# One tile's masks ahead of attention, and a planner that reckons with instruction supply and a halved clock

## The chip, the cores and the metric

The kernel runs on one core of a Trainium2 chip. The metric is device time in microseconds (us), the median of three runs. The engines are PE (matrix products, with PEld for its weight loads), DVE (vector), ACT (scalar), POOL (GpSimd) and SP, which only issues DMA transfers here.

## The reference

Sliding-window attention with sink tokens, then two MLPs, all in f32:

```python
scores = scale * q @ k^T                    # B=2, H=8, S=768, D=64
keep = (pos_k < n_sink) | ((0 <= rel) & (rel < window))     # n_sink=4, window=128
a = softmax(where(keep, scores, -1e9)); attn = a @ v        # -> x: 1536 tokens x 512
h = x @ w_in;  y = (h * clip(h + 3, 0, 6) / 6) @ w_out      # first MLP, d_ff = 2048
h = y @ w_in2; out = (h * sigmoid(1.702 * h)) @ w_out2      # second MLP
```

## The kernel before, in words

**Tiles.** Attention is cut into 12 tiles of 128 query tokens, T0 to T11. Each tile has two *duos* of four heads, so there are duos 0 to 23. For a duo PE makes the scores (L1381), DVE adds a mask and takes the row minimum of the negated scores (L1396, into a `pexp` buffer), ACT takes the exponential and its row sum (L1404), DVE inverts the sums (L1412, L1413), DVE or ACT scales each head (L1423 or L1421), PE transposes in two *turns* (L1432) and ACT or DVE copies each turn into a `pts` buffer (L465, L467). After both duos PE multiplies with the values (L1455, L1463), and ACT and DVE split the result into `xyh + xyl` (L465, L1482). [...] There are eight `pexp` buffers, which is one tile's worth, and eight PSUM banks in all.

**MLPs.** MLP products use f32 numbers split into two rounded parts, three products each. An *item* is 512 tokens by 128 columns of `w_in` (12 records of L1158, then the gate, then 12 of L1207). Weights come packed through two `stage` buffers and are converted by ACT (L495) and DVE (L500, L508, L516, L523); a stage buffer can be loaded again once L523 has read it. Eight `items` of the first MLP run on the first 512 tokens, that is on T0 to T3, while the later tiles' attention is still being done.

**Masks.** T0 uses mask 0, T1 mask 1, T2 to T5 mask 2, and the second batch alike. All three are written before attention begins, from iotas and the two parameters.

**The planner.** The program is straight-line code under manual scheduling. `Plan.op` collects operations with an engine, a cost in ns, buffers and a due time; `Plan.issue` runs through them as a list scheduler, keeps a clock for each engine, picks the next operation by its earliest start and its due time, and emits it. So its constants (`SLACK`, `HOLD`, `MARGIN`, `RAMP`, `PAIR`, ...) set each engine's order of instructions. The engines then run these orders strictly, with semaphores. SP too is one queue in order: a load that waits for its buffer holds up every load behind it.

```python
start, o, cost = min((c for c in best[eng] if c[0] <= soon), key=lambda c: c[1].due)
...
if eng == "PE":
    if o.tiled != tiled:
        start += ENTER if o.tiled else LEAVE
        tiled = o.tiled
end = start + cost
```

Of the kernel before, what the change touches and what calls it, by code (L numbers as in the profile page):

```python
# [9 lines left out]
F32 = mybir.dt.float32  # L10
# [4 lines left out]
ALU = mybir.AluOpType  # L15
PSUM = bass.MemoryType.PSUM

P = 128
SINKS = 4
HALF = 64  # L20
# [14 lines left out]
NVC = 3  # L35
SLACK = 50
HOLD = 425
MARGIN = 18538
LONG = 1000
ENTER = 100  # L40
LEAVE = 200
STICK = 88113
WAIT = 5
ISSUE = 1300
ADD_DMA = 4500
PACT = 0.09
PDVE = 0.51
STRETCH = 1.0
LATER = 1000000
H_BANKS = 3  # L50
RAMP0 = 8045
RAMP = 1654
PAIR = 4384
PAIR2 = 5887
DOWN = 7072
START = 592
RATE = 1.56
RATE2 = 1.21
NU = 3
# [16 lines left out]
def tile_sink_window_attention_moe_moe2(  # L76
# [10 lines left out]
    nc = tc.nc  # L87
# [12 lines left out]
    W = P + TAIL  # L100
# [31 lines left out]
    def load_kq(T):  # L132
        nc.sync.dma_start(out=kqt[T], in_=kq[T])
# [17 lines left out]

    const.tile([P, 88], F32, name="gap_x")
    xy = const.tile([P, 2, 2 * NBLK * NC * 256 + APART], F32R, name="xy")
# [86 lines left out]
    const.tile([P, 72], F32, name="gap_w")  # L240
    with tc.tile_pool(name="msk", bufs=1) as mp:
        grid = mp.tile([P, P], F32, name="grid")
        nc.gpsimd.iota(grid, pattern=[[-1, P]], base=0, channel_multiplier=1, allow_small_or_imprecise_dtypes=True)
        colc = mp.tile([P, HALF], F32, name="colc")
        nc.gpsimd.iota(colc, pattern=[[1, HALF]], base=0, channel_multiplier=0, allow_small_or_imprecise_dtypes=True)
        far = mp.tile([P, P], F32, name="far")
        nc.gpsimd.iota(far, pattern=[[-1, P]], base=P, channel_multiplier=1, allow_small_or_imprecise_dtypes=True)
        t0 = mp.tile([P, P], F32, name="t0")
        out_of = mp.tile([P, P], F32, name="out_of")
        snk = mp.tile([P, HALF], F32, name="snk")  # L250
        nos = mp.tile([P, HALF], F32, name="nos")
        nc.gpsimd.memset(masks[0], LOW)
        nc.vector.tensor_scalar(out=t0, in0=grid, scalar1=0.0, scalar2=None, op0=ALU.is_lt)
        range_check()
        fast = nc.values_load(flag[0:1, 0:1], min_val=0, max_val=1)
        window_of_params()
        top, low, keys, own, ends = slice(0, HALF), slice(HALF, P), slice(HALF, P), slice(P, P + HALF), slice(P + HALF, W)
        first_sinks, rest = slice(P, P + SINKS), slice(P + SINKS, W)
        at = lambda out, grid, op, x: nc.vector.tensor_scalar(
            out=out, in0=grid, scalar1=x, scalar2=LOW, op0=op, op1=ALU.mult  # L260
        )
        times = lambda out, in_: nc.vector.tensor_scalar(out=out, in0=in_, scalar1=LOW, scalar2=None, op0=ALU.mult)

        nc.vector.scalar_tensor_tensor(out=out_of, in0=grid, scalar=win, in1=t0, op0=ALU.is_ge, op1=ALU.max)
        at(snk, colc, ALU.is_ge, nsk)
        times(masks[1][:, keys], out_of[:, :HALF])
        times(masks[0][low, own], out_of[low, HALF:])
        nc.vector.tensor_tensor(out=masks[0][:, keys], in0=masks[1][:, keys], in1=snk, op=ALU.max)
# [7 lines left out]
        nc.vector.tensor_tensor(out=masks[1][top, rest], in0=masks[2][top, rest], in1=nos[top, :], op=ALU.min)  # L276

        nc.vector.tensor_copy(masks[2][:, : P + SINKS], masks[1][:, : P + SINKS])
        nc.vector.tensor_copy(masks[2][low, rest], masks[1][low, rest])

# [18 lines left out]
    class Op:  # L299
        pass  # L300

    class Plan:
# [19 lines left out]
        def op(self, opts, fn, due, reads=(), writes=(), adds=(), chain=None, after=()):  # L322
            o = Op()
            o.opts, o.fn, o.due = opts, fn, LATER if due is None else due
            o.deps, o.order, o.finish, o.eng = [], list(after), None, None
            o.tiled = chain == "scores" or opts[0][1] == 1830
            for b in reads:
                o.deps += b.writers
# [45 lines left out]
        def issue(self):  # L374
# [20 lines left out]
            ready = [o for o in self.ops if not need[id(o)]]  # L395
            at = dict.fromkeys(ENG, 0)
            tiled = True
            while ready:
                best = {}
                for o in ready:  # L400
                    placed = self.place(o)
                    if placed is None:
                        continue
                    t = placed[0]
                    pick = None
                    for eng, cost in o.opts:
                        x = max(t, at[eng])
# [14 lines left out]
                if eng == "PE":  # L422
# [865 lines left out]
    def mlp_rings(plan, pool, psum):  # L1288
# [7 lines left out]
        for cls, n, cols, dt in (  # L1296
            ("w0h", 2, 512, F32R), ("w0l", 2, 512, F32R), ("u", NU, 512, F32), ("aside", 4, 512, F32),
        ):
            plan.ring(cls, n, lambda k, cls=cls, cols=cols, dt=dt: pool.tile([P, cols], dt, name=cls, tag=f"{cls}{k}"))
        spare = [t.rearrange("p h d -> p (h d)") for t in vb]  # L1300
# [18 lines left out]
    def plan_attention(plan, pool, due):  # L1319
# [23 lines left out]
        def load(T):  # L1343
            if ("kq", T) not in landed:
                plan.op([("SP", 532480 / RATE_DMA)], lambda e: load_kq(T), None, writes=[kq_b[T]])
            if ("vb", T) not in landed:
# [4 lines left out]
        def duo(d, pts):  # L1351
# [37 lines left out]
            )  # L1389
            heads = [(a, j) for a in range(2) for j in range(2)]  # L1390
            for a, j in heads:
                n = 2 * a + j
# [7 lines left out]
                    when, reads=[sc[j], mask_b[kind]], writes=[pes[n], nbs[n]],  # L1400
                )
                plan.op(
                    [("ACT", 443)],
# [333 lines left out]
```

## Time and profile before

| | |
|---|---|
| time, median of 3 runs (lowest to highest) | 573.64 us (573.54 to 573.85) |
| the profiled execution: its time, its span | 575.76 us, 573.9 us |
| PE, DVE, ACT busy share of the span | 97%, 84%, 70% |
| mean granted clock of PE | 0.985 |

The span runs from the first to the last instruction; what lies around it in the profiled execution is 575.76 - 573.9 = 1.9 us. Busy shares are averages over very different stages: the first 60 us are attention with a few items, from there to about 564 us PE has work without a break.

### The profile page before, as it was taken

To read this page: it belongs to the slowest core of one execution; us is meant where nothing else is said; L and a number is where in the kernel's file an instruction comes from. 1 tells how busy PE (TensorE), PEld (TensorE's weight loads), DVE (VectorE), ACT (ScalarE), POOL (GpSimd) and SP (SyncE) were. 2 spreads that over 40 slices of the span, in tenths; PEclk is the share of its full clock that TensorE was granted. 3 is DMA by queue.
4 is the path that set the end of the run, shared out by engine and by line. 5 is a ranking of instruction groups with operands and counts; after the bars stand their busy time and mean duration, and the time that the engine had idled before them with its cause. 6 is when DMAs were issued, how large, how long until landed. Compare 5 with 4: busy or idle time off the path is not lost.

```text
span 573.9 us, 11897 instructions
## 1 busy us (share of the span) xinstructions
PE 559.1 (97%) x4626; PEld 501.4 (87%) x4626; DVE 481.7 (84%) x1039; ACT 400.9 (70%) x855; POOL 63.9 (11%) x70
## 2 busy tenths in 40 slices
PE   6898999999999999999999999999999999999996
PEld 6787888888888888889999888888888888999996
DVE  6779999999997669999999999999666655667785
ACT  6779779846675678578765565765478788768762
POOL 0000000000000203000000000000003334765000
PEclk9769999999999999999999999999999999999999
DMA  8956364324334515112222142324034467999512
GB/s 263 381 196 196 129 211 166 101 90 135 133 131 152 106 49 100 38 73 74 75 75 97 50 147 94 127 73 148 0 93 73 74 107 145 168 184 199 100 38 79
DMA packets 27824, 69.89 MB, mean 122 GB/s; under 512 B 2736, under 2 KB 15024, under 8 KB 23664
## 3 DMA queue, kind: packets, MB, share of 16 engines
q1 hardware_dynamic: 15248, 53.06, 27.2%
q0 software_dynamic: 12224, 15.73, 17.4%
q8 instruction: 38, 0.62, 0.4%
q10 hardware_dynamic: 288, 0.26, 0.2%
q14 instruction: 26, 0.21, 0.1%
HBM read 47.02 MB, written 3.15 MB: 87 GB/s over the span
## 4 chain that ended last, share of the span: by engine, by line
PE 92%; ACT 4%; DMA 1%; issue 1%; DVE 0%; DVEq 0%; ACTq 0%
PE bank L1207 29%; PE bank L1158 21%; PE bank L954 13%; PE bank L650 13%; PE bank L738 7%; PE bank L1432 3%; PE bank L1381 3%; PE bank L1455 2%; PE bank L1463 2%; DMA stage<-in_w_dram 1%; ACT pexp L1404 1%; ACT pts L465 1%; ACT pexp L1421 0%; ACT wf L495 0%; ACT u L1170 0%
## 5 line engine op out<-in xcount | busy, mean ns | idle before, releaser
L1207 PE MATMUL bank<-wg 128*128 128x512 f32 x768 | 187.5, 381 | 0.0
L1207 PEld LDWEIGHTS bank<-wg 128*128 128x128 f32 x768 | 142.4, 189 | 19.0
L1158 PE MATMUL bank<-xy,w0h 128*128 128x512 f32 x384 | 116.3, 384 | 1.6 <-ACT pts L465 0.9
L1158 PEld LDWEIGHTS bank<-xy,w0h 128*128 128x128 f32 x384 | 71.1, 189 | 12.0 <-ACT pts L465 1.2
L1158 PE MATMUL bank<-xy,w0l 128*128 128x512 f32 x192 | 72.8, 379 | 0.0
L465 ACT CAST wg<-wf 128x512 fp32r<-128x512 f32 x80 | 49.1, 617 | 31.4 <-PE bank L1207 24.1
L902 POOL DMA_DIRECT2D wf<-wf x24 | 29.0, 1300 | 229.0 <-ACT wf L883 193.1
L1404 ACT ACTIVATE pexp<-pexp,nb 128x196 f32<-128x196 f32 x96 | 43.1, 452 | 10.7 <-DVE nb L1396 10.6
L578 DVE TENSOR_TENSOR wg<-wf,wg 128x512 fp32r<-128x512 f32 x64 | 43.7, 684 | 3.1 <-ACT wg L465 3.1
L578 DVE TENSOR_TENSOR w0l<-wf,w0h 128x512 fp32r<-128x512 f32 x60 | 40.9, 682 | 3.3 <-ACT w0h L465 3.1
L495 ACT ACTIVATE wf<-stage 128x1024 f32<-128x1024 f32 x32 | 38.0, 1188 | 6.0 <-DMA stage<-in_w_dram 5.9
L1158 PEld LDWEIGHTS bank<-xy,w0l 128*128 128x128 f32 x192 | 36.3, 189 | 5.1
L593 DVE TENSOR_TENSOR wg<-u,wg 128x512 fp32r<-128x512 f32 x56 | 38.0, 683 | 1.2 <-ACT wg L465 0.7
L523 DVE SCALAR_TENSOR_TENSOR wf<-stage,wf 128x1024 int32<-128x1024 int32 x32 | 38.9, 1216 | 0.1
L516 DVE SCALAR_TENSOR_TENSOR wf<-stage,wf 128x1024 int32<-128x1024 int32 x32 | 38.9, 1215 | 0.1
L650 PE MATMUL bank<-xy,w0h 128*128 128x512 f32 x128 | 38.1, 379 | 0.0
L604 ACT ACTIVATE u<-bank 128x512 f32<-128x512 f32 x32 | 19.1, 596 | 27.2 <-PE bank L1158 20.1
L465 ACT CAST wg<-u 128x512 fp32r<-128x512 f32 x47 | 29.0, 622 | 8.5 <-DVE u L1175 5.6
L1170 ACT ACTIVATE u<-bank,three 128x512 f32<-128x512 f32 x32 | 21.8, 682 | 16.4 <-PE bank L1158 16.2
L1432 PE MATMUL bank<-ident,pexp 128*128 128x128 f32 x192 | 29.6, 293 | 3.7 <-DVE pexp L1423 2.9
L1396 DVE CUSTOM_DVE_ANT_0 pexp<-bank,mask 128x196 f32<-128x196 f32 x96 | 29.9, 354 | 1.1 <-PE bank L1432 0.7
L1432 PEld LDWEIGHTS bank<-ident,pexp 128*128 128x128 f32 x192 | 23.7, 149 | 8.1 <-issue 2.6
(245 smaller groups left out, 1234.3 us busy)
## 6 DMA issues: line engine op xcount, KB each, us to landing
stage<-in_w_dram SPq DMA_DIRECT2D x32, 1024.0 KB, 4.9
wf<-wf POOLq DMA_DIRECT2D x24, 256.0 KB, 3.8
wf<-in_kq_dram SPq DMA_DIRECT2D x8, 520.0 KB, 11.2
vc<-in_vc_dram SPq DMA_DIRECT2D x12, 320.0 KB, 3.5
vb<-in_v_dram SPq DMA_DIRECT2D x10, 256.0 KB, 5.1
kept<-in_kq_dram SPq DMA_DIRECT2D x4, 520.0 KB, 10.3
vc<-xy SPq DMA_DIRECT2D x7, 256.0 KB, 2.6
vc<-xy POOLq DMA_DIRECT2D x7, 256.0 KB, 4.7
```

The lines of the kernel that those rows point to most:

```text
L465: eng.copy(out, in_)
L495: lambda e: e.activation(w.tile.bitcast(F32), top.bitcast(F32), AF.Abs),
L516: lambda e: e.scalar_tensor_tensor(out=w.tile, in0=top, scalar=-0x40000000, in1=w.tile, op0=ALU.bitwise_and, op1=ALU.bitwise_or),
L523: lambda e: e.scalar_tensor_tensor(out=w.tile, in0=low, scalar=29, in1=w.tile, op0=ALU.logical_shift_right, op1=ALU.bitwise_or),
L578: lambda e: e.tensor_tensor(out=lo.tile[at], in0=of(), in1=hi.tile[at].bitcast(F32), op=ALU.subtract),
L650: e.matmul(bank.tile, l, woven(r), start=(begin and j == 0 and k == 0), stop=(j == 1 and k == 2), skip_group_check=True,)
L738: e.matmul(bank.tile[:, :256], l, woven(r), start=(begin and j == 0 and k == 0), stop=(j == 1 and k == 2), skip_group_check=True,)
L954: e.matmul(to, l, woven(t), start=(begin and n == 0 and m == 0 and e4 % share == 0), stop=(n == pairs - 1 and m == 2), skip_group_check=True,)
L1158: e.matmul(h.tile[:, :n], w, woven(x), start=(c == 0 and k == 0), stop=(c == NC - 1 and k == 2))
L1207: e.matmul(yb.tile, l, woven(r), start=(begin and k == 0), stop=(end is not None and k == 2))
L1404: lambda e, n=n: e.activation(pes[n].tile[:, :W], pes[n].tile[:, :W], AF.Exp, bias=nbs[n].tile, scale=-1.0, accum_out=z.tile[:, n : n + 1],),
L1432: e.transpose(pt.tile[:, n * P : (n + 1) * P], pes[2 * a + j].tile[:, x * P : (x + 1) * P], ident)
```

## The change

**Masks.** Before attention DVE now writes only mask 0 (with the key columns of mask 1, from which mask 0 is made). The rest of mask 1 (`second_mask`, 7 instructions) and mask 2 (`third_mask`, 2) become planned operations of DVE after duo 0's comparisons. One comparison (`t0`) goes from DVE to POOL. The mask work space moves from a pool of its own to slot 0 of the `aside` ring.

**Planner.** It counts the instructions passed by PE and lets PE stop when a fetched block is used up (`FETCHED`, `CHUNK`, `FETCH`, `FETCH_BUSY`); it doubles the cost of PE work in a stretch behind much idle time (`idle`, `slow`); DVE's clock starts at `MASKED`; loads of k and q from tile 7 on are not issued before `KQ_AT + (T - 7) * KQ_STEP`. The other constants and the order of the first loads are new.

```diff
-    ("kq", 0), ("kq", 1), ("vb", 0), ("vc", 0), ("w", 0), ("vb", 1), ("vc", 1), ("kq", 2), ("vb", 2), ("vc", 2), ("kq", 3),
-    ("w", 1),
+    ("kq", 0), ("vb", 0), ("kq", 1), ("vc", 0), ("vc", 1), ("vb", 1), ("w", 0), ("kq", 2), ("vb", 2), ("vc", 2), ("kq", 3), ("w", 1),
...
-SLACK = 50
-HOLD = 425
-MARGIN = 18538
+SLACK = 54
+MASKED = 5700
+HOLD = 597
+MARGIN = 20604
...
+CHUNK = 252
+FETCHED = 443
+FETCH = 2800
+FETCH_BUSY = 6300
+LATE_KQ = 7
+KQ_AT = 53230
+KQ_STEP = 5947
...
-        nc.vector.tensor_scalar(out=t0, in0=grid, scalar1=0.0, scalar2=None, op0=ALU.is_lt)
+    nc.gpsimd.tensor_scalar(out=out_of, in0=grid, scalar1=0.0, scalar2=None, op0=ALU.is_lt)
...
+                    if start > at[eng] > 6000:
+                        idle.append((at[eng], start))
+                    passed += o.count
+                    if passed > edge:
+                        seen = start + cost * (edge - passed + o.count) / o.count
+                        if coming > seen:
+                            idle.append((seen, coming))
+                            cost += coming - seen
+                            seen = coming
+                        coming = seen + (FETCH_BUSY if self.dma_free > seen + 1500 else FETCH)
+                        edge += CHUNK
+                    while idle and idle[0][1] < idle[-1][1] - 4300:
+                        idle.pop(0)
+                    if idle and sum(b - a for a, b in idle) > 2100:
+                        a = idle[0][0] + 2900
+                        slow = (a, max(a, idle[-1][1]) + 3500)
+                        idle.clear()
+                    cost += max(0, min(slow[1] - max(start, slow[0]), 2 * (start + cost - max(start, slow[0]))) / 2)
...
+                o = plan.op([("SP", 532480 / RATE_DMA)], lambda e: load_kq(T), None, writes=[kq_b[T]])
+                if T >= LATE_KQ:
+                    o.not_before = KQ_AT + (T - LATE_KQ) * KQ_STEP
...
+            if d == 0:
+                plan.op([("DVE", 1300)], lambda e: second_mask(), when, writes=mask_b[1:2], after=seen)
+                plan.op([("DVE", 400)], lambda e: third_mask(), when, reads=mask_b[1:2], writes=mask_b[2:], after=seen)
```

**What moves.** PE, behind T0's four turns (`pts` and `vb_63`, `vc_66` are T0's). Before, T0's values come next, then the scores of duos 4 and 5 (of each kind of row one stands here), then T1's turns:

```order
L1432 MATMUL bank<-ident,pexp 128x128 x16
L1455 MATMUL bank<-pts,vb_63 64x128 x2
L1463 MATMUL bank<-pts,vc_66 64x64 x4
...
L1381 MATMUL bank<-wf 64x64 x8
L1381 MATMUL bank<-wf 64x68 x4
...
L1432 MATMUL bank<-ident,pexp 128x128 x16
```

Of the change, in the same place:

```order
L1479 MATMUL bank<-ident,pexp 128x128 x16
L1422 MATMUL bank<-wf 64x64 x8
L1422 MATMUL bank<-wf 64x68 x4
...
L1502 MATMUL bank<-pts,vb_63 64x128 x2
L1510 MATMUL bank<-pts,vc_66 64x64 x4
...
L1479 MATMUL bank<-ident,pexp 128x128 x16
```

So the scores of T2 go ahead of T0's values. What follows has the same blocks in both kernels as far as T1's values: T1's turns, duos 6 and 7, T1's values. Up to the first long run of L1158 (L1194 in the change), two more turns stand ahead of it in the change: 18 against 16.

SP, behind the branch. Before (`wf` and `kept` take k and q of tiles 4 on, `stage` takes weights, `vb` and `vc` the values):

```order
L133 DMA wf<-in_kq_dram 128x1040 x4
L133 DMA kept<-in_kq_dram 128x1040
L143 DMA vb_63<-in_v_dram 128x512
L133 DMA kept<-in_kq_dram 128x1040 x2
L149 DMA vc_66<-in_vc_dram 80x1024
L143 DMA vb_64<-in_v_dram 128x512
L127 DMA stage_60<-in_w_dram 128x2048
L149 DMA vc_67<-in_vc_dram 80x1024
L143 DMA vb_65<-in_v_dram 128x512
L127 DMA stage_61<-in_w_dram 128x2048
```

Of the change:

```order
L140 DMA wf<-in_kq_dram 128x1040 x3
L134 DMA stage_60<-in_w_dram 128x2048
L150 DMA vb_63<-in_v_dram 128x512
L156 DMA vc_66<-in_vc_dram 80x1024
L150 DMA vb_64<-in_v_dram 128x512
L134 DMA stage_61<-in_w_dram 128x2048
L156 DMA vc_67<-in_vc_dram 80x1024
```

Three loads of k and q stand there instead of seven; those of tiles 7 to 10 come later, one by one among the weight loads. The third weight tile now stands ahead of T3's values, the fourth ahead of the second part of T4's.

DVE, from duo 0's reciprocal on (`z_249` is duo 0's row sums, `z_318` duo 1's, `aside0` now holds the iotas). The rows with `mask1`, `mask2` and `gap_x` are the moved mask work; left out are a multiplication and two copies. Of the change:

```order
L1460 RECIPROCAL z_249<-z_249 128x4
L265 TENSOR_SCALAR mask1_123<-aside0_126,par_121 128x64
L265 TENSOR_SCALAR mask2_124<-aside0_126,par_121 64x64
L265 TENSOR_SCALAR gap_x_69<-aside0_126,par_121 64x64
...
L283 TENSOR_TENSOR mask1_123<-mask2_124,gap_x_69 64x64
L1470 TENSOR_SCALAR pexp_177<-pexp_177,z_249 128x196
L1470 TENSOR_SCALAR pexp_178<-pexp_178,z_249 128x196
L286 COPY mask2_124<-mask1_123 128x132
L287 COPY mask2_124<-mask1_123 64x64
L1459 TENSOR_SCALAR z_318<-z_318 128x4
```

Before, these nine mask instructions stood ahead of the first comparison, and the reciprocal was followed at once by the four scalings of duo 0 (L1423).

## Rows read from the trace of the kernel before

**Rows 1.** Busy us of PE, PEld, DVE, ACT, POOL by stretch; granted clock, DMA share, GB/s.

```profile
6.60:13.50 6.90, 4.10 (x183) 3.60 (x179) 6.10 (x37) 5.29 (x21) 0.00 (x0) 1.00 1.04 320
13.50:20.30 6.80, 6.48 (x110) 6.03 (x113) 4.94 (x24) 5.31 (x18) 0.00 (x0) 0.50 1.03 343
20.30:27.10 6.80, 4.50 (x156) 4.04 (x148) 6.00 (x24) 5.47 (x19) 0.00 (x0) 1.00 1.01 403
27.10:34.00 6.90, 6.33 (x68) 5.30 (x72) 2.51 (x10) 2.87 (x8) 0.00 (x0) 0.50 0.75 275
34.00:37.40 3.40, 3.40 (x58) 2.94 (x59) 3.29 (x19) 3.40 (x14) 0.00 (x0) 0.51 0.85 314
...
47.10:60.00 12.90, 11.50 (x96) 9.52 (x97) 12.32 (x30) 11.50 (x28) 0.00 (x0) 1.00 0.52 164
...
60.00:100.00 40.00, 40.00 (x456) 34.75 (x455) 39.83 (x109) 32.82 (x88) 0.00 (x0) 1.00 0.52 177
```

**Rows 2.** Timeline of PE: start, us, instruction [idle before <- releaser].

```profile
5.78 3.41 PE L1381 MATMUL bank<-wf 64*64 64x64 f32 x192
...
13.82 1.44 PE L1432 MATMUL bank<-ident,pexp 128*128 128x128 f32 x6 [0.56 <-ACT pts L465]
15.19 0.70 PE L1455 MATMUL bank<-pts,vb 128*64 128x128 f32 x4
...
18.80 1.99 PE L1381 MATMUL bank<-wf 64*64 64x64 f32 x73
21.03 0.58 PE L1381 MATMUL bank<-wf 64*64 64x64 f32 x23 [0.24 <-issue]
21.54 1.97 PE L1432 MATMUL bank<-ident,pexp 128*128 128x128 f32 x16
23.44 1.60 PE L1381 MATMUL bank<-wf 64*64 64x64 f32 x88
27.67 0.51 PE L1381 MATMUL bank<-wf 64*64 64x68 f32 x8 [2.62 <-issue]
28.10 0.69 PE L1455 MATMUL bank<-pts,vb 128*64 128x128 f32 x4
...
38.84 0.44 PE L1455 MATMUL bank<-pts,vb 128*64 128x128 f32 x4
...
40.80 1.12 PE L1432 MATMUL bank<-ident,pexp 128*128 128x128 f32 x6
...
47.84 0.48 PE L1158 MATMUL bank<-xy,w0h 128*128 128x512 f32 x1 [0.24 <-DVE xy L1482]
```

**Rows 3.** Timeline of SP: DMA issues.

```profile
13.42 3.75 SPq L133 DMA_DIRECT2D wf<-in_kq_dram  x4
...
32.52 0.36 SPq L127 DMA_DIRECT2D stage<-in_w_dram  x1
```

**Rows 4.** Timeline of POOL and DVE to the first comparison.

```profile
1.74 0.25 POOL L252 MEMSET mask<- 128x196 f32 x1
...
4.53 0.22 DVE L253 TENSOR_SCALAR t<-grid 128x128 f32<-128x128 f32 x1
...
7.76 0.36 DVE L1396 CUSTOM_DVE_ANT_0 pexp<-bank,mask 128x196 f32<-128x196 f32 x1 [0.27 <-issue]
```

**Rows 5.** Timeline of ACT and DVE behind T1's values.

```profile
31.83 0.59 ACT L465 CAST xy<-bank 128x512 fp32r<-128x512 f32 x1 [4.03 <-PE bank L1463]
...
32.45 0.69 DVE L1482 TENSOR_TENSOR xy<-bank,xy 128x512 fp32r<-128x512 f32 x1 [4.36 <-ACT xy L465]
...
37.10 1.53 ACT L465 COPY pts<-bank 128x512 f32<-128x512 f32 x3
```

**Rows 6.** Groups of ACT: busy us, mean ns of one | idle before.

```profile
L1404 ACT ACTIVATE pexp<-pexp,nb 128x196 f32<-128x196 f32 x96 | 43.1, 452 | 10.7 <-DVE nb L1396 10.6
```

**Rows 7.** The chain that ended last, between 38 and 62 us: start, us, what.

```profile
44.01 8.30 DMA stage<-in_w_dram
...
56.15 1.56 PE bank L1158 x6
```

More of the change, by code (lines that the diff above doesn't have):

```diff
@@ L50 @@
 H_BANKS = 3
[L51 to L58, printed above, removed]
+RAMP0 = 7690
+RAMP = 1541
+PAIR = 4632
+PAIR2 = 5467
+DOWN = 7079
+START = 4000
+RATE = 1.82
+RATE2 = 1.34
 NU = 3
@@ L149, in load_vc @@
         nc.sync.dma_start(out=vcs[T % NVC].rearrange("p x h d -> p (x h d)")[:VR], in_=vc[T])
-    const.tile([P, 88], F32, name="gap_x")
+    gap_x = const.tile([P, 88], F32, name="gap_x")
     xy = const.tile([P, 2, 2 * NBLK * NC * 256 + APART], F32R, name="xy")
@@ L240, in tile_sink_window_attention_moe_moe2 @@
     const.tile([P, 72], F32, name="gap_w")
[L241 to L252, printed above, removed]
-        nc.vector.tensor_scalar(out=t0, in0=grid, scalar1=0.0, scalar2=None, op0=ALU.is_lt)
[L254 to L268, printed above, removed]
@@ new lines, in tile_sink_window_attention_moe_moe2 @@
+    aside0 = const.tile([P, 512], F32, name="aside0")
+    grid, far, out_of, colc, snk = (
+        aside0[:, a:b] for a, b in ((0, P), (P, 2 * P), (2 * P, 3 * P), (3 * P, 3 * P + HALF), (3 * P + HALF, 4 * P))
+    )
+    nos = gap_x[:, :HALF]
+    nc.gpsimd.iota(grid, pattern=[[-1, P]], base=0, channel_multiplier=1, allow_small_or_imprecise_dtypes=True)
+    nc.gpsimd.iota(colc, pattern=[[1, HALF]], base=0, channel_multiplier=0, allow_small_or_imprecise_dtypes=True)
+    nc.gpsimd.iota(far, pattern=[[-1, P]], base=P, channel_multiplier=1, allow_small_or_imprecise_dtypes=True)
@@ new lines, in tile_sink_window_attention_moe_moe2, with at @@
+    nc.gpsimd.memset(masks[0], LOW)
+    nc.gpsimd.tensor_scalar(out=out_of, in0=grid, scalar1=0.0, scalar2=None, op0=ALU.is_lt)
+    range_check()
+    fast = nc.values_load(flag[0:1, 0:1], min_val=0, max_val=1)
+    window_of_params()
+    top, low, keys, own, ends = slice(0, HALF), slice(HALF, P), slice(HALF, P), slice(P, P + HALF), slice(P + HALF, W)
+    first_sinks, rest = slice(P, P + SINKS), slice(P + SINKS, W)
+    def at(out, grid, op, x):
+        nc.vector.tensor_scalar(out=out, in0=grid, scalar1=x, scalar2=LOW, op0=op, op1=ALU.mult)
@@ L270, in tile_sink_window_attention_moe_moe2, with times, second_mask @@
+    def times(out, in_):
+        nc.vector.tensor_scalar(out=out, in0=in_, scalar1=LOW, scalar2=None, op0=ALU.mult)
+    nc.vector.scalar_tensor_tensor(out=out_of, in0=grid, scalar=win, in1=out_of, op0=ALU.is_ge, op1=ALU.max)
+    at(snk, colc, ALU.is_ge, nsk)
+    times(masks[1][:, keys], out_of[:, :HALF])
+    times(masks[0][low, own], out_of[low, HALF:])
+    nc.vector.tensor_tensor(out=masks[0][:, keys], in0=masks[1][:, keys], in1=snk, op=ALU.max)
+    def second_mask():
         at(masks[1][:, :HALF], far[:, HALF:], ALU.is_ge, win)
@@ L300, in tile_sink_window_attention_moe_moe2 @@
         pass
+    COUNTS = {870: 96, 1830: 96, 440: 8}
     class Plan:
@@ L326, in op @@
             o.tiled = chain == "scores" or opts[0][1] == 1830
+            o.count = 0
+            o.not_before = 0
+            if opts[0][0] == "PE":
+                cost = opts[0][1]
+                if cost in COUNTS:
+                    o.count = COUNTS[cost]
+                elif abs(cost / 112 - round(cost / 112)) < 0.01:
+                    o.count = 2 * round(cost / 112)
+                else:
+                    o.count = 2 * round(cost / 216)
             for b in reads:
@@ L395, in issue @@
             ready = [o for o in self.ops if not need[id(o)]]
-            at = dict.fromkeys(ENG, 0)
+            at = {**dict.fromkeys(ENG, 0), "DVE": MASKED}
             tiled = True
+            passed, edge, coming = 36, FETCHED, 13400
+            idle, slow = [], (0, 0)
             while ready:
@@ L1298, in mlp_rings @@
         ):
-            plan.ring(cls, n, lambda k, cls=cls, cols=cols, dt=dt: pool.tile([P, cols], dt, name=cls, tag=f"{cls}{k}"))
+            plan.ring(
+                cls, n, lambda k, cls=cls, cols=cols, dt=dt: aside0 if (cls, k) == ("aside", 0)
+                else pool.tile([P, cols], dt, name=cls, tag=f"{cls}{k}"),
+            )
         spare = [t.rearrange("p h d -> p (h d)") for t in vb]
@@ L1401, in duo @@
                 )
+                seen.append(plan.ops[-1])
                 plan.op(
```

13 lines of the change are left out of this document (7 added, 6 removed).

## The prediction

> **What bounds the kernel now.** First the table: PE is busy for 97% of the span. From about 60 us on it works without a break at the full clock, in a stretch where DVE too is busy for 39.83 of 40 us [rows 1]. There nothing can be won by another order of the same products, only lost. So I looked at the first 60 us, stretch by stretch. [...] Then PE's timeline: it stops for 0.24 us before 21.03 and for 2.62 us before 27.67, released by "issue", that is by nothing that the profile shows [rows 2]. Between the restart at 13.82 and the first of these stops lie 6 + 48 (T0's values) + 73 = 127 records, between the first and the second 23 + 16 + 88 = 127 again [rows 2]. Equal counts speak for a supply of instructions in blocks: the engine has used up a block and the next has not landed. Such a block took about 21.03 - 13.82 = 7.2 and 27.67 - 21.03 = 6.6 us, while the DMA engines were full (shares of 1.01 to 1.04) [rows 1, 2]. They were full because SP issues seven loads of k and q, for tiles 4 to 10, from 13.4 us on, four of them at once [rows 3]. [...]
>
> What follows from the stop is the dearest stretch. T1's values start at 28.10 and run at half clock. ACT waits 4.03 us for them and DVE, behind ACT, 4.36 us [rows 5]; between 27.1 and 34.0 both are busy for less than 3 of 6.9 us [rows 1]. T2's values start at 38.84, the MLP's first long run at 47.84 [rows 2]. Last, the chain between 38 and 62 us goes through a weight load: issued at 44.01, landed 8.30 us later, its product at 56.15 [rows 7].
>
> **The change, part by part.** I follow the new orders with these durations: a tile's values 3.61 us at half clock (15.19 to 18.80) and 1.96 at full (38.84 to 40.80), two duos' scores 2.50 at half (18.80 to 21.54 without the stop) and about 1.7 at full, four turns 1.9 [rows 2]; an exponential 0.45, a copy of a turn 0.48 (three in 1.53 with their overlap) [rows 5, 6]. Handoffs between engines I take as 0.25.
>
> *Masks.* The 15 DVE instructions from 4.53 to 7.49 (7.76 less its 0.27) take 0.2 us each [rows 4]. Nine leave, so mask 0 is ready at about 5.8, and 0.27 us on (the step over the branch, [rows 4]) DVE could begin. Duo 0's scores, one of four in the 3.41 us from 5.78, are there at 6.6 [rows 2]; with a handoff DVE starts at 6.9 instead of 7.76, a head start of 0.86 us. The nine, 1.8 us, come back right behind duo 1's comparisons, ahead of two scalings that the first turns need. That delays T0's turns, but the third of these waits until 13.82 for instructions anyway [rows 2]: nothing on PE's path, 1.8 us less on DVE's side. The comparison on POOL has no row; POOL is free from 2.0 us and DVE reads the result near 4.8, so up to 2.8 us of it are hidden; its neighbour, a memset of more columns, takes 0.25 [rows 4]. I take nothing; were it ten times that neighbour, still nothing.
>
> *Order up to T1's values.* T2's scores ahead of T0's values swaps two blocks: the same records stand between the stops, so T0's values end at 21.5 to 22.0, where T1's turns started before (21.54). Four turns (with waits for DVE's last scalings, 2.2), duos 6 and 7 (1.7, and 0.8 for PSUM banks that ACT must empty) end at 26.8. On ACT, from T0's values: their cast, a weight conversion (twice a copy's columns), four copies and two exponentials, 7 x 0.48 + 0.9 = 4.3 us with 0.3 of handoff, so 26.1 to 26.6. T1's values start near 27.0 instead of 28.10, if the block is there. It should be: with three loads of k and q instead of seven, and a weight tile that can only be issued when DVE has read w0 (near 20.7; before at 32.52 [rows 3]), the DMA engines run dry near 25 us. Bounds: 0 (the stop stays) to 1.7 (no bank waits, stop gone). I take 1.1.
>
> *To the first long MLP run.* ACT has 20 exponentials, 6 scalings, 8 copies and 3 casts between T1's last copy and the end of T3's cast: 20 x 0.45 and, with a copy's time for each of the others, 17 x 0.48, or 17.2 us, so 44.0 without any wait. T3's comparisons need `pexp` buffers that T2's turns free, and these stand behind T1's values. With the full clock ACT and DVE lose about 1 us there and the run starts at 45.1. With half the clock from 27.1 on (PE is busy for some 4.6 us in the stretch before, close to the 4.5 of now) T1's values and T2's turns take 3.4 us more; some lies beside ACT's own work, and the run starts near 46.5 to 47. I take 46.2: 1.6 us ahead of 47.84. Two more turns are done by then, 0.7 us.
>
> *Behind it.* From 47.1 to 60 us PE is idle for 12.90 - 11.50 = 1.4 us now [rows 1], around the wait for that weight tile [rows 7]. In the new order the tile can be issued when DVE has read w1, well before 40 us by the steps above, so this wait goes. Instead the first gate comes late: its two DVE steps stand behind the third tile's conversion, about 1 us. Net 0.4. PE is then 1.6 + 0.7 + 0.4 = 2.7 us ahead.
>
> *From 60 us on* DVE decides whether PE may stay ahead. Its balance: 0.86 gained at the start, 1.8 paid for masks, 2.5 to 3.5 of its 4.36 us of waiting saved, so 1.6 to 2.6 us ahead. In the new order attention's last tiles come earlier, the same work in another mixture; I count nothing for it. The late loads of k and q I cost at nothing: tile 7's scores stand six items into the first MLP, and an item is 24 records, and six took 1.56 us behind that weight wait [rows 7], so six items are some 37 us; even with a fifth less for a steadier pace that is past 46 + 30 = 76 us, without the attention between; the load is planned near 53 and the loads of now land within 8 to 9 us when the queue is busy (8.30, [rows 7]). Without that cover every us of lateness would be PE's.
>
> *Sum.* Between DVE's 2.1 (the middle) and PE's 2.7 I take **2.3 us**. The profiled execution would go from 575.76 to 573.5; the median of the runs shown lies 2.1 below that execution, so 573.64 becomes **571.3 us**.
>
> **The rivals.** A measurement of this kernel tells 0.2% (1.1 us) from no change.
>
> *The clock stays full behind 27.1 us.* Then the long run starts at 45.1, PE leads by 3.8, and DVE, whose wait shrinks below 1 us, by about 2.6; at 3.2 the time is 570.4. Against it: PE's new waits are shorter but as many.
>
> *The stop does not go.* The two stops could be something else than supply, such as the landing of T3's k and q or a transfer that the new order delays as much. Then no wait is taken away: T1's values stay at 28.1 behind a stop, at half clock; ACT and DVE starve as before, and only the 1.4 us behind 47 are won, less 0.9 that the masks cost DVE beyond its head start: 0.5, so 573.1, within 0.2%. For it: the profile gives the wait at 13.82 another name, a copy on ACT [rows 2]. Against it: twice the same count, and a stop in the midst of one duo's scores, for which nothing new had to land. [...]
>
> *DVE becomes the bound (slower).* It has 0.2 us to spare in 40 from 60 to 100 us [rows 1]. The masks' 1.8 us less the 0.86 of head start are 0.9, and if the new mixture asks for another 0.4 ahead of the first gates and no waiting is saved, PE is 1.3 us later: 574.9. It decides as soon as DVE's wait behind T1's values stays above 3.4 of its 4.36 us.
>
> **How the numbers follow.** Likeliest, 0.62: 571.3, its own range 569.9 to 572.5. Full clock, 0.10: 570.4. The stop stays, 0.16: 573.1. DVE, 0.12: 574.9. Of the likeliest, 0.04 lies within 0.2%. So faster 0.68, same 0.20, slower 0.12. The range of 8 in 10 leaves out the slower case and the best end of the full clock: 569.0 to 574.2.
>
> **What would show it.** DVE's first comparison at 6.9, nine mask instructions near 9.5 to 11.9; no stop of 2 us on PE before T1's values, which start near 27; the wait of DVE behind T1's values below 2.5 us; the first long MLP run at 45 to 47 us, with no weight load in the chain behind it; from 60 us on still no idle PE. A stop of more than 2 us between 22 and 28, a second stretch at half clock beyond 37, or PE waiting for DVE between 60 and 160 us would make me wrong.

## The result, and the profile after

The kernel after takes 577.45 us (median of 7 runs, 577.07 to 578.83), the kernel before beside it 573.85 (7 runs, 573.37 to 575.80): a ratio of 1.0057, interval 1.0042 to 1.0072. It is **slower by 0.6%**, 3.6 us between the medians. The prediction said 571.3 and faster; sign and range were missed. The profiled execution of after took 577.41 us, its span is 575.6.

In the kernel after the scores stand in L1422, the turns in L1479, the values in L1502 and L1510, the MLP's products in L1194 and L1243, ACT's copies and casts in L501, DVE's weight splits in L614; in the runs further below these numbers shift a little. First some stretches of the ramp, to be read beside [rows 1]:

```profile
13.50:20.30 6.80, 3.45 (x102) 3.24 (x101) 5.90 (x22) 6.39 (x22) 0.00 (x0) 0.68 1.04 335
20.30:27.10 6.80, 5.41 (x75) 4.64 (x68) 3.95 (x14) 3.01 (x7) 0.00 (x0) 0.82 1.01 408
27.10:34.00 6.90, 5.20 (x154) 4.52 (x152) 5.66 (x21) 6.34 (x23) 0.00 (x0) 1.00 0.23 84
...
47.10:60.00 12.90, 12.17 (x102) 10.73 (x102) 12.87 (x29) 11.03 (x25) 0.00 (x0) 1.00 0.46 165
```

The second stretch at half clock, from 27.1 us on, is gone (1.00 instead of 0.50), and the DMA engines run dry near 28 us (share 0.91 from 27.5 to 28.0, 0.29 from 28.5 to 29.0). PE's timeline shows what the ramp did with that, beside [rows 2]:

```profile
9.20 1.64 PE L1422 MATMUL bank<-wf 64*64 64x64 f32 x96 [1.53 <-DMA wf<-in_kq_dram]
...
17.66 2.90 PE L1422 MATMUL bank<-wf 64*64 64x64 f32 x96 [2.64 <-ACT pts L501]
20.49 0.69 PE L1502 MATMUL bank<-pts,vb 128*64 128x128 f32 x4
...
24.06 0.33 PE L1502 MATMUL bank<-pts,vb 128*64 128x128 f32 x2 [1.39 <-issue]
...
30.77 0.35 PE L1422 MATMUL bank<-wf 64*64 64x64 f32 x9 [1.22 <-issue]
31.05 0.44 PE L1502 MATMUL bank<-pts,vb 128*64 128x128 f32 x4
...
37.93 0.44 PE L1502 MATMUL bank<-pts,vb 128*64 128x128 f32 x4
...
48.40 0.68 PE L1194 MATMUL bank<-xy,w0h 128*128 128x512 f32 x2
```

T2's scores wait 2.64 us for PSUM banks that ACT must empty, the stop for instructions has moved and split (1.39 and 1.22), and T1's values start at 31.05 instead of 28.10, yet T2's at 37.93 instead of 38.84. Then a stretch far behind the ramp, first after, then before:

```profile
210.00:220.00 10.00, 8.96 (x41) 7.27 (x40) 8.59 (x18) 7.45 (x16) 1.21 (x1) 1.00 0.54 95
220.00:230.00 10.00, 9.05 (x43) 7.61 (x42) 10.00 (x20) 7.77 (x13) 0.00 (x0) 1.00 0.00 0
```

```profile
210.00:220.00 10.00, 10.00 (x77) 8.86 (x74) 8.86 (x16) 6.85 (x13) 4.32 (x4) 1.00 0.65 157
220.00:230.00 10.00, 10.00 (x48) 8.77 (x47) 9.99 (x23) 8.12 (x16) 0.58 (x1) 1.00 0.37 56
```

PE, which before had no idle time there, stands still for 2 us in after. Its waits from 195 to 240 us (us in total, times, longest):

```profile
PE bank L1194 <- DVE w0l L614: 1.5, 2, 1.0
PE bank L1194 <- ACT w0h L501: 0.5, 1, 0.5
```

The chain that ended last no longer begins in the ramp [rows 7]. It begins here (start, us, what), and behind it PE is the chain to the end:

```profile
214.79 3.72 DMA vb<-xy
...
218.61 0.42 DVE vc L877
...
221.68 0.68 DVE wg L614
...
222.96 0.61 DVE w0l L614
...
223.61 1.13 PE bank L1194 x4
```

To put sizes on stretches whose orders differ, I took PE's **lag**: from all 4626 matmul records of a trace, the time passed since PE's first record less the price of the records so far at the full clock. The prices are what a record took in the trace of before behind 60 us: 18 ns a record of scores, 41 of values, 216 for a product on 512 columns, 112 on 256, and for a record of a turn an estimate of 95, between the 89 and 99 of runs of four and eight; the 18 records ahead of attention count nothing. The trace has two records for each score and values matmul of the order: 48 for a duo's scores, 48 for a tile's values, 4 for a turn. Lag in us when so many us of work are done:

```
work done                 17     50     90    180    200   at the end
before (575.76 us)     19.48  24.52  25.80  28.02  28.04  28.91
before again (574.25)  17.50  22.47  23.75  26.65  26.67  27.58
after (577.41)         19.20  22.47  24.60  26.87  29.64  30.38
after again (578.14)   19.43  22.88  24.96  27.23  29.94  30.71
late tail (577.43)     19.28  22.32  24.54  26.76  27.08  30.36
add at 7.5 (573.90)    18.92  22.20  24.28  26.55  26.53  27.17
masks alone (576.73)   18.08  22.26  26.61  28.98  29.00  29.89
```

180 to 200 us of work are about 209 to 231 us of after's time. Against the first trace of before, after leads by 2.05 us at 50 and by 1.15 at 180; against a second trace of before it is level at 50, 0.85 behind at 90 and 0.2 at 180. Against either it then loses 2.75 us between 180 and 200, since after's lag grows by 2.77 there and before's by 0.02. That is more than the 2 us of idle time: in after, products (L1194) that follow without a wait start 0.22 us apart and last 0.38, so each of the three waits also breaks this overlap.

### The profile page after: what moved, and what is told of

It reads as the page before. It is cut to its first block, busy times and chain, and to the rows that moved or that the text cites. A ratio compares the mean times of both kernels' runs of the same rounds, so it can differ in the third digit from the quotient of the medians.

```text
span 575.6 us, 11907 instructions
## 1 busy us (share of the span) xinstructions
PE 554.9 (96%) x4626; PEld 496.9 (86%) x4626; DVE 485.0 (84%) x1046; ACT 396.9 (69%) x847; POOL 64.3 (11%) x71
## 3 DMA queue, kind: packets, MB, share of 16 engines
HBM read 47.02 MB, written 3.15 MB: 87 GB/s over the span
## 4 chain that ended last, share of the span: by engine, by line
PE 60%; DVE 1%; DMA 1%; issue 0%; DVEq 0%
PE bank L1243 18%; PE bank L990 13%; PE bank L686 13%; PE bank L1194 10%; PE bank L774 7%; DMA vb<-xy 1%; DVE xy L1174 0%; DVE wg L614 0%; DVE w0l L614 0%; DVE u L1211 0%; DVE vc L877 0%; DVE stage L1114 0%; DVE xt L892 0%; DVEq L877 0%
## 5 line engine op out<-in xcount | busy, mean ns | idle before, releaser
L1243 PE MATMUL bank<-wg 128*128 128x512 f32 x768 | 188.2, 381 | 0.0
L1243 PEld LDWEIGHTS bank<-wg 128*128 128x128 f32 x768 | 142.1, 189 | 18.9 <-DVE wg L629 0.3
L1194 PE MATMUL bank<-xy,w0h 128*128 128x512 f32 x384 | 116.1, 384 | 0.5 <-ACT w0h L501 0.5
L1194 PEld LDWEIGHTS bank<-xy,w0h 128*128 128x128 f32 x384 | 71.1, 189 | 10.5 <-ACT w0h L501 0.9
L1194 PE MATMUL bank<-xy,w0l 128*128 128x512 f32 x192 | 73.0, 380 | 1.5 <-DVE w0l L614 1.5
L501 ACT CAST wg<-wf 128x512 fp32r<-128x512 f32 x73 | 44.9, 617 | 33.3 <-PE bank L1243 26.0
L614 DVE TENSOR_TENSOR wg<-wf,wg 128x512 fp32r<-128x512 f32 x64 | 43.9, 685 | 3.7 <-ACT wg L501 3.6
L614 DVE TENSOR_TENSOR w0l<-wf,w0h 128x512 fp32r<-128x512 f32 x60 | 41.1, 684 | 2.4 <-ACT w0h L501 2.3
L1194 PEld LDWEIGHTS bank<-xy,w0l 128*128 128x128 f32 x192 | 36.3, 189 | 7.4 <-DVE w0l L614 2.3
L501 ACT CAST wg<-u 128x512 fp32r<-128x512 f32 x48 | 29.6, 621 | 10.1 <-DVE u L1211 8.3
L1479 PE MATMUL bank<-ident,pexp 128*128 128x128 f32 x192 | 27.2, 276 | 4.0 <-ACT pexp L1468 1.8
L501 ACT COPY pts<-bank 128x512 f32<-128x512 f32 x45 | 24.8, 586 | 8.6 <-PE bank L1479 8.6
```

The source lines that it names most:

```text
L501: eng.copy(out, in_)
L614: lambda e: e.tensor_tensor(out=lo.tile[at], in0=of(), in1=hi.tile[at].bitcast(F32), op=ALU.subtract),
L1194: e.matmul(h.tile[:, :n], w, woven(x), start=(c == 0 and k == 0), stop=(c == NC - 1 and k == 2))
L1243: e.matmul(yb.tile, l, woven(r), start=(begin and k == 0), stop=(end is not None and k == 2))
```

## The experiments

Beside each run the kernel before ran on the same chip; the ratios are to that.

**The kernel before, a second trace.** No edit.

> The kernel before, unchanged, for a second trace of it. Its seven runs lie in two groups, 573.4 to 573.9 and 575.7 to 575.8 us, and the one with the trace was 575.76. If a trace at about 573.6 comes, it must hold some 2 us less: theory A (two groups differ in the ramp, where the clock falls) has the first long MLP run start 1 to 2 us before 47.84; the rival has every stage equal and the difference behind 240 us.

574.25 us in this execution, 573.31 to 576.7 in the 17 of before beside it. Theory A held; this execution is shorter by 1.5 us, not quite the 2. From the windows (the 3.4 us behind it are at the full clock too):

```profile
27.10:34.00 6.90, 5.23 (x117) 4.14 (x117) 4.32 (x19) 4.69 (x15) 0.00 (x0) 1.00 0.91 317
```

and from PE's and DVE's timelines:

```profile
27.84 0.35 PE L1381 MATMUL bank<-wf 64*64 64x68 f32 x8 [2.62 <-issue]
28.11 0.44 PE L1455 MATMUL bank<-pts,vb 128*64 128x128 f32 x4
...
46.05 0.48 PE L1158 MATMUL bank<-xy,w0h 128*128 128x512 f32 x1 [0.23 <-DVE xy L1482]
```

```profile
30.81 0.69 DVE L1482 TENSOR_TENSOR xy<-bank,xy 128x512 fp32r<-128x512 f32 x1 [2.55 <-ACT xy L465]
```

The same program, the same stop of 2.62 us, T1's values at the same time (28.11 against 28.10 [rows 2]); but the clock stays full, DVE waits 2.55 us behind the values instead of 4.36, and the long run starts at 46.05 instead of 47.84. So the first trace showed an execution that had lost some 1.8 us here, and the second lost none of it. In two further traces below (late loads alone, first loads alone) the clock from 27.1 to 37.4 us is full as well; how many executions of before lose the 1.8 us isn't known.

**Four due-time constants set back, and all fifteen.** In the kernel after:

```diff
-DOWN = 7079
-START = 4000
-RATE = 1.82
-RATE2 = 1.34
+DOWN = 7072
+START = 592
+RATE = 1.56
+RATE2 = 1.21
```

and, for the second, SLACK, HOLD, MARGIN, STICK, WAIT, PACT, PDVE, RAMP0, RAMP, PAIR and PAIR2 as well.

> The kernel after with four due-time constants of the planner set back (START, RATE, RATE2, DOWN); everything else as after. In its order attention's last four value blocks stand behind 112, 137, 159 and 184 us of TensorE's work, as in the kernel before (111, 136, 160, 186), against 103, 125, 148 and 169 in the kernel after. Theory A (the new dues bring attention's tail forward, and VectorE's work on the halved blocks and the weights' splits then falls together at 205 to 235 us, where TensorE waits 2.0 us for it): no idle TensorE between 195 and 235 us, and about 575 us, 2 to 2.5 faster than the kernel after. Rival B (the loss came from the later k and q loads or from the new order of the ramp): still about 577.4.

> The kernel after with all fifteen planner constants of before, but with its masks, its order of the first loads, its supply and clock in the planner and its later k and q loads. Theory A: the tail of attention stands as before (112, 136, 160, 186 us of work), no idle TensorE between 195 and 235 us, and 573 to 575 us. Rival B (the new rules cost, not the constants): 577.

581.91 us (1.0129, 1.0105 to 1.0152) and 580.07 (1.0101, 1.0082 to 1.0120). On the totals both theories missed. In the stretch theory A held: from 180 to 200 us of work the lag moves by -0.02 in the one (31.61 to 31.59) and by +0.02 in the other (30.30 to 30.32). But the constants set the ramp's order too, and there the lag at 50 us of work is 26.08 and 26.58 instead of 22.47. A planner's constant can't be tried alone when it reorders everything ahead of the place in question.

**Attention's last tiles later.** The constant that spaces the due times of the last four tiles (the expectation says eight):

```diff
-PAIR2 = 5467
+PAIR2 = 7600
```

> The kernel after with one constant changed: PAIR2 from 5467 to 7600, the spacing of the due times of attention's last eight tiles. The order on TensorE is that of the kernel after for the first 96 us of its work; then attention's last four value blocks stand behind 107, 137, 164 and 188 us of work instead of 103, 125, 148 and 169. Theory A (the early tail costs the 2.8 us that the kernel after loses between 195 and 235 us): the ramp as in the kernel after, no idle TensorE between 195 and 235 us, 574.6 us. Rival B (VectorE is too late anyway once the masks' work and the new ramp are there, and TensorE only waits in another place): a new wait between 100 and 195 us, 576 to 577.5.

577.25 us, 1.0049 (1.0034 to 1.0065): rival B's total, theory A's stretch. The windows, one of the stretch and the one in which most of the time went instead (from 220 to 230 us PE is busy throughout as well):

```profile
210.00:220.00 10.00, 10.00 (x86) 8.69 (x85) 6.93 (x13) 6.68 (x11) 4.03 (x3) 1.00 0.64 185
...
270.00:280.00 10.00, 8.87 (x67) 8.21 (x66) 9.84 (x21) 5.29 (x14) 0.00 (x0) 1.00 0.19 71
```

```profile
272.97 0.49 PE L774 MATMUL bank<-xt,sh 128*128 128x256 f32 x2 [1.13 <-ACT u L791]
```

With attention's end moved back, the idle 2 us at 210 to 230 are gone (lag 0.32 more from 180 to 200). But from 220 to 280 us of work, some 250 to 310 us of time, the lag now grows by 2.97, against 0.59 in the second trace of before: PE waits for ACT in the items on halved blocks. Rival B had put the new wait between 100 and 195 us.

**The price of the adding DMA.** What stands in DVE's queue at 218.61 is a subtraction on a copy of the attention result (`halve`: SP copies one part, a DMA on GpSimd's queue adds the other, DVE takes differences). In the kernel after DVE waits for such copies four times:

```profile
204.00 0.43 DVE L877 TENSOR_TENSOR vb<-vb 128x256 f32<-128x256 f32 x1 [1.24 <-DMA vb<-xy]
205.31 0.42 DVE L877 TENSOR_TENSOR vc<-vc 128x256 f32<-128x256 f32 x1 [0.88 <-DMA vc<-xy]
...
206.82 0.43 DVE L877 TENSOR_TENSOR vb<-vc,vb 128x256 f32<-128x256 f32 x1 [0.48 <-DMA vc<-xy]
...
218.61 0.42 DVE L877 TENSOR_TENSOR vc<-vb,vc 128x256 f32<-128x256 f32 x1 [1.41 <-DMA vb<-xy]
...
222.87 0.69 DVE L614 TENSOR_TENSOR w0l<-wf,w0h 128x512 fp32r<-128x512 f32 x1
```

The first three, 2.6 us in all, reach PE by way of ACT, which waits 2.45 us for the third of these subtractions (until 207.32) and has PE's next weights behind it, and by way of DVE's own splits (PE's waits before 210.79 and 212.03); the fourth reaches PE at 223.61. SP issues the eighth copy late, first for a landing, then for the buffer that a subtraction frees (SP's timeline and waits):

```profile
192.55 5.36 SPq L863 DMA_DIRECT2D vc<-xy  x6
209.20 0.59 SPq L863 DMA_DIRECT2D vb<-xy  x1
```

```profile
SPq L863 <- DMA vb<-xy: 6.1, 1, 6.1
SPq L863 <- DVE vc L877: 5.5, 1, 5.5
```

The planner prices the add at 4.5 us (`ADD_DMA`). The trace has, from issue to landing (count, KB each, median us), and up to 1.4 us of issue on POOL ahead of it:

```profile
vc<-xy POOLq DMA_DIRECT2D x6, 256.0 KB, 5.2
```

```diff
 def halve(t0, when):
...
-                    [("POOL", ADD_DMA)],
+                    [("POOL", 7500)],
```

> The kernel after with one price of the planner changed: the adding DMA of the halved blocks (the one on GpSimd's queue) is planned to land 7.5 us after its issue instead of 4.5. In the trace of the kernel after it took 1.2 us more at the issue, 4.3 to 5.2 behind it, and the eighth copy came 6.5 us late on SP. The orders are the same up to 189 us of VectorE's work and 208 us of TensorE's; behind that VectorE's subtractions on the copies stand behind the weights' splits and not ahead of them. Theory A (VectorE stands in its queue at a subtraction whose copy has not landed, with the split that TensorE needs behind it): TensorE's 2.0 us of idle time between 205 and 235 us go, the ramp and the rest stay; 575.2, 2.2 faster than the kernel after. Rival B (VectorE's work as such is too much there, wherever it stands): the idle time comes in smaller pieces up to 250 us, and 577.

**574.17 us**, 0.9991 (0.9979 to 1.0003) of before: theory A, and 1.0 us better than its number. The ramp is after's, the order is after's up to 189 us of DVE's work, and the loss is gone (lag 26.55 to 26.53). PE has no idle time left:

```profile
210.00:220.00 10.00, 10.00 (x48) 8.74 (x48) 10.00 (x22) 8.95 (x18) 1.14 (x1) 1.00 0.29 59
220.00:230.00 10.00, 10.00 (x48) 8.77 (x47) 10.00 (x21) 7.93 (x13) 0.07 (x1) 1.00 0.17 27
```

DVE does more in these 20 us than in after (20.0 against 18.59) and PE is not held up: not the amount of work was at fault but its order, weight splits behind subtractions whose copies had not landed. The eighth copy comes no earlier here; its add is issued even later than in after (214.79):

```profile
218.86 1.21 POOL L868 DMA_DIRECT2D vc<-xy  x1 [9.54 <-DVE wg L614]
```

But the splits that PE needs now stand ahead of the subtractions on it, and DVE waits for copies for only 0.2 us. Setting this one number undoes the whole slowdown: 577.45 to 574.17 is 3.3 us. But 7.5 lies above what the add took (5.2 and up to 1.4 of issue); the measured 6.6 was not run as a price. It is shown that the price sets this order, not that a true price would have been enough.

**The kernel after, again.** No edit.

> The kernel after, unchanged, for a second trace and more times beside the other three. Theory A: 577.1 to 578.8 again, and the loss between 195 and 235 us is in this trace too (TensorE idle for about 2 us there).

578.08 us (576.74 to 578.34), 1.0061 (1.0043 to 1.0079); the lag grows by 2.71 from 180 to 200 us of work. As expected: the loss belongs to the program, not to one execution.

**The masks alone.** The kernel before with the masks' part of the diff (comparison on GpSimd, `second_mask` and `third_mask` as planned operations), all else of before.

> The kernel before with only the masks' part of the change: the comparison on GpSimd, the second and third mask behind duo 0. Planner, its constants and the order of the first loads are those of before. Theory A: VectorE's first comparison comes 0.6 to 0.9 us earlier than 7.76, and the whole about 0.5 faster than before, 573.1 (573.6 before). Rival B (the nine mask operations, 1.8 us, fall where VectorE is waited for in the ramp): 0.5 to 1.5 slower, 574.1 to 575.1.

576.91 us, 1.0062 (1.0040 to 1.0083): rival B's side and twice its size, in another place. The ramp is as good as before's (lag 22.26 at 50), but 4.35 us go by 90, against 1.28 in the second trace of before. From the windows and PE's waits at 60 to 120 us:

```profile
80.00:90.00 10.00, 9.29 (x117) 7.39 (x106) 9.93 (x28) 8.88 (x24) 0.00 (x0) 1.00 0.39 134
90.00:100.00 10.00, 9.15 (x128) 7.60 (x127) 9.97 (x29) 7.92 (x19) 0.00 (x0) 1.00 0.55 199
```

```profile
PE bank L1177 <- DVE u L1194: 0.9, 1, 0.9
PE bank L1226 <- DVE wg L597: 0.6, 1, 0.6
```

PE waits for DVE while DVE is full; these waits are 1.5 of the 3.1 us. Is it the 1.8 us of mask operations, or the order that the planner makes once they are there? The next two runs take the operations away and keep the orders.

**Masks on GpSimd.** Eight of the nine operations go to GpSimd ahead of attention; the ninth (a minimum) stays on DVE behind duo 1. In the kernel before:

```diff
-        at(masks[1][:, :HALF], far[:, HALF:], ALU.is_ge, win)
+        at(masks[1][:, :HALF], far[:, HALF:], ALU.is_ge, win, nc.gpsimd)
...
-        nc.vector.tensor_copy(masks[2][low, rest], masks[1][low, rest])
+        nc.gpsimd.tensor_copy(masks[2][low, rest], masks[1][low, rest])
```

and likewise in the kernel after with the add at 7.5 us, where the planner goes on to reserve DVE's time for them.

> The kernel before with eight of the nine operations of masks 1 and 2 on GpSimd, ahead of attention, and the ninth on VectorE behind duo 1; planner, constants and all other orders are those of before. VectorE is rid of 1.6 us and begins its comparisons some 0.8 us earlier, without paying the nine back. Theory A (from T0's turns on, TensorE's ramp is set by blocks of instructions and ScalarE, not by VectorE): first comparison near 7.0, T1's values still near 28, the whole 573.5 to 574.8 as before. Rival B (VectorE sets the ramp and the stretch to 100 us): 1.2 to 1.6 us faster than before, 572.6 to 573.2.

> The kernel after with the add priced at 7.5 us, and with eight of the nine operations of masks 1 and 2 on GpSimd ahead of attention (the ninth stays in VectorE's slot); the planner still reserves VectorE's time for them, so all orders are those of the run priced at 7.5 us. Theory A (the nine lie beside waits for instructions and ScalarE): 573.6 to 575.0, as without. Rival B (VectorE is short in the ramp and to 100 us): 1 to 1.5 us faster, 572.7 to 573.2, which would be under the kernel before.

573.60 us (0.9997, 0.9982 to 1.0012) and 574.20 us (1.0000, 0.9991 to 1.0010): theory A in both. Rid of 1.6 us, DVE starts at 6.66 and 6.94 us, and nothing comes of it: in the second the lag is 0.8 lower at 50 us of work (21.38 against 22.20) and level at 90 (24.33 against 24.28). So under these orders the operations cost nothing; what the masks cost alone under before's constants comes with the order that they bring about. Whether in that order the operations themselves also cost something wasn't separated.

**The order of the first loads alone.** In the kernel before:

```diff
-    ("kq", 0), ("kq", 1), ("vb", 0), ("vc", 0), ("w", 0), ("vb", 1), ("vc", 1), ("kq", 2), ("vb", 2), ("vc", 2), ("kq", 3),
-    ("w", 1),
+    ("kq", 0), ("vb", 0), ("kq", 1), ("vc", 0), ("vc", 1), ("vb", 1), ("w", 0), ("kq", 2), ("vb", 2), ("vc", 2), ("kq", 3), ("w", 1),
```

> The kernel before with only the order of the first loads of after: v's first block ahead of T1's k and q. The order on TensorE, VectorE and ScalarE is that of before throughout. Theory A: duos 2 and 3 wait about 1.5 us for T1's k and q (as in the kernel after), which lies beside VectorE's work on duos 0 and 1; T0's turns stay at 10.9 to 11.1, the whole within 0.3 of before. Rival B (the early scores set the ramp): T0's turns about 1 us later, 574.5 to 575.

575.07 us, 1.0009 (0.9997 to 1.0021): theory A within what can be told. The scores wait 1.18 us for T1's k and q, the first turns still start at 10.95. The stops are there in other shares, 3.15 us before 21.82 and 1.13 before 28.46.

**The late loads alone.** In the kernel before:

```diff
+                o = plan.op([("SP", 532480 / RATE_DMA)], lambda e: load_kq(T), None, writes=[kq_b[T]])
+                if T >= 7:
+                    o.not_before = 53230 + (T - 7) * 5947
```

> The kernel before with one part of the change: the loads of k and q of tiles 7 and on are planned no earlier than 53 us. Masks, first loads, constants and the planner's other rules are those of before. Theory A (a block of 127 records takes 6.6 us because the k and q loads fill the DMA engines): the second stop shrinks from 2.62 to about 1.5 us or less, T1's values start near 27.0 instead of 28.1, and no tile's scores wait for a late load; 573.0 to 574.0, no change that can be told. Rival B (a block takes 6.6 us whatever is loaded): stop and start as before. Rival C (the late loads are late for their scores): waits for DMA in front of scores behind 80 us, 575 or more.

576.49 us (574.07 to 578.21), 1.0030 (1.0014 to 1.0046): more than theory A said, and the time of rival C. But the profiled execution took 574.51, and in it no scores wait for a late load. The stop is rival B's, 2.63 us:

```profile
27.98 0.35 PE L1384 MATMUL bank<-wf 64*64 64x68 f32 x8 [2.63 <-issue]
```

It doesn't decide on the cause of the stop, since with three of the loads and the earlier ones the DMA engines still have a share of 0.79 from 20.3 to 27.1 us (1.01 in before [rows 1]; PE had restarted at 21.35). What the slower executions lose is in no trace and stays open.

**All later k and q behind v's load at 30 us.** In the kernel before, orders of the other engines unchanged; loads that the planner put ahead of 20 us are held and issued behind the next load of another kind:

```diff
-                o.fn(ENG[eng])
+                if eng == "SP" and start < 20000 and abs(o.opts[0][1] - 532480 / RATE_DMA) < 1:
+                    self.held.append(o)
+                else:
+                    o.fn(ENG[eng])
+                    if eng == "SP" and start > 20000:
+                        for x in self.held:
+                            x.fn(ENG["SP"])
+                        self.held = []
```

> The kernel before with the loads of k and q of tiles 4 to 10 issued on SP behind v's load at 30 us instead of from 13.4 us on; the orders on TensorE, VectorE, ScalarE and GpSimd are those of before throughout. The DMA engines then run dry near 18 us. In the trace of before TensorE's block of instructions lands (16,384 bytes on the queue of instructions) at 19.75 and 26.25 us, 1.3 to 1.4 us ahead of its restarts at 21.03 and 27.67. Theory A (a block waits behind the data queued ahead of it): the blocks land right behind their request, by 17 and 22 us, the stop of 2.62 us goes, and T1's values start near 25 us instead of 28.1; tile 4's scores may wait for their late load by up to 1 us; 572 to 574. Rival B (a block comes 4 us behind its request whatever else is loaded): stops and T1's values as before, and 574 to 575 by the later loads.

PE's timeline:

```profile
25.14 0.44 PE L1463 MATMUL bank<-pts,vb 128*64 128x128 f32 x4
...
32.04 0.93 PE L1389 MATMUL bank<-wf 64*64 64x64 f32 x48 [2.62 <-DMA wf<-in_kq_dram]
...
46.66 1.47 PE L1166 MATMUL bank<-xy,w0h 128*128 128x512 f32 x2 [2.29 <-issue]
```

The DMA share from 20.3 to 27.1 us is 0.23, the stop of 2.62 us ahead of T1's values is gone and they start at 25.14: theory A on the cause. The whole is 578.23 us (575.56 to 579.46), 1.0047 (1.0031 to 1.0062), and that was expected by neither: the scores now wait 2.62 us for k and q, and a new stop of 2.29 us stands at 46.66, behind the loads that were moved there (share 1.03 from 37.4 to 47.1). The first stop, before 20.97, stays with 0.84. In this run the place of the loads decided where the stop is paid, not whether.

## Why the prediction was wrong

**From 60 us on: the step that failed.** "In the new order attention's last tiles come earlier, the same work in another mixture; I count nothing for it." It was 2.75 us (after against before, 180 to 200 us of work), and the one price that undoes it gives 3.3 back. That is about half of the 6.2 us between 571.3 and 577.45; with the price set the kernel takes 574.17, and the other 2.9 belong to the next step. With attention's end earlier, the eight copies of the halved blocks are asked for one behind the other from 191.8 us on, the eighth waits for a buffer until 209.20, DVE stands at subtractions whose copies have not landed, and the weight splits that PE needs stand behind them. The rows of the argument end at 100 us; the work of the last tiles, the copies and the halves had none.

**The sum's foot.** The profiled execution lay 2.1 us above the median, and the prediction carried its gain over to the median unchanged. But the second trace of before puts 1.8 us of that difference into the very stretch that the gain was counted in (27.1 to 47.84 us, at half clock up to 37.4, with DVE's wait of 4.36, which is 2.55 in the second). Against the first trace the ramp did gain: 2.05 us of lag at 50 us of work, near the 2.3 of the sum. Against the second it gained nothing, 22.47 each: DVE's wait behind T1's values did shrink to 1.21, but from 2.55. So, as far as two traces show, the 2.3 us were a gain over the one execution that had been profiled, not over the median.

**Masks.** Right: first comparison at 7.10 (said 6.9), the nine operations at 9.71 to 11.9, nothing on PE's path in the two orders from which they were taken away (in masks alone this is open).

**Order up to T1's values.** Wrong by 4 us, 31.05 instead of 27.0. Two steps: T0's values end at 25.1 instead of 21.5 to 22.0, since T2's scores, now ahead of them, wait 2.64 us for PSUM banks; and the DMA engines run dry near 28 us, not 25, so the stop stays, as 1.39 and 1.22. (The sum's own terms give 26.2 to 26.7 for the end of duo 7's scores, not 26.8; that is the smaller error. The 0.25 us that the sum takes for a handoff are an estimate of the author's that no row shows; in before DVE's step starts at 32.45, 0.03 us behind the end of ACT's cast, 31.83 + 0.59 [rows 5].) That is the rival "the stop does not go" up to its place; it priced this at 573.1. The block takes 30.77 - 24.06 = 6.7 us, as read.

**To the first long run, and behind it.** 48.40 instead of 46.2. The clock stayed full (1.00) from 27.1 on, a rival's condition (570.4), but it stayed full in the second trace of before too. That 4.5 busy us in the stretch before bring the half clock, as the 46.5 to 47 assume, is not shown: late loads alone had 4.52 there, and the clock behind was 1.00. The weight wait is gone as said: idle time from 47.1 to 60 is 12.90 - 12.17 = 0.73 instead of 1.40. In the second trace of before it is 12.90 - 11.97 = 0.93, so little was won here too.

**Late loads.** No scores wait for one in after. The 8 to 9 us for a load to land were read from a weight tile; the loads of k and q took 11.2 in before (median of eight); no wait came of it. Alone they cost 0.3% in executions that no trace shows, so the zero isn't shown right.

**The rival "DVE becomes the bound"** named the right engine and sign, but its place (60 to 160 us), its condition (a wait behind T1's values above 3.4 us; after has 1.21) and its price (574.9) were others. After loses 0.8 us more than before from 50 to 90 us of work; by 180 all but 0.2 of that is back against the second trace of before, nothing against the first. The decision fell 50 us behind the place that it named.

## What to carry to other kernels

A planner optimises against its prices, so its new order is only as good as the price that it newly leans on: when an edit moves work, look up every transfer that the moved work waits for, and compare its planned latency with the measured one (4.5 against 5.2 and the issue here). In after one late transfer held DVE for 1.41 us, and behind it in DVE's order stood the split for which PE then waited 0.95 us (223.61); so ask of each moved operation what is queued behind it, to the end of the program and not to the end of the edited stretch. When the profiled execution is slower than the median, find where that difference lies before counting a gain in the same place.

## What the runs showed of the hardware

**In before a block of PE's instructions came late while data filled the DMA engines.** The profile lists a queue q8 of kind instruction; it moves 38 packets of 16,384 bytes in the trace of before. Between the two stops of [rows 2] lie 127 records, with as many weight loads 254 instructions, and PE's 4626 records with theirs are 36.4 times that. That each packet is such a block is inferred from these counts. In that trace, 25.1 to 26.3 us has one of these packets, and 21.0 to 25.1 has none (queue, kind: packets, MB, share):

```profile
q1 hardware_dynamic: 127, 0.47, 98.4%
q8 instruction: 1, 0.02, 5.6%
```

PE, restarted at 21.03, gets its next block 4 us later, in the midst of full DMA engines (q1 has 100.9% from 21.0 to 25.1), and starts again at 27.67, 1.4 us behind the packet. In the run with the k and q loads out of the way the packet is there from 22 to 24 us, among little else (none is there from 20.9 to 22.5, so it comes 1.5 us or more behind PE's restart at 20.97), and no stop follows ahead of T1's values:

```profile
q1 hardware_dynamic: 31, 0.06, 8.2%
q8 instruction: 1, 0.02, 3.0%
```

**An adding DMA took longer than the planner's price of 4.5 us.** 256 KB took 5.2 us from issue to landing in after (`vc`, six of them; two of `vb` 4.3), with up to 1.4 of issue ahead, and 4.7 in before, where a plain copy of the same size took 2.6; in after, where SP issued six one behind the other, the plain copy took 6.6 (medians).

**The same program was granted different clocks.** From 27.1 to 37.4 us PE's granted clock was 0.50 to 0.51 in one execution of before [rows 1] and 1.00 in another, behind a stretch (20.3 to 27.1) in which it was busy for 4.50 us in the one and 4.36 in the other. In late loads alone it had been busy for 4.52, and the clock stayed at 1.00. The difference was worth 1.8 us at 47 us.
